# Running the feed-forward blocks of finished rows inside the attention phase of a one-core kernel

## The chip, the cores and the metric

The kernel runs on one core of a Trainium2 chip. The metric is the device time of one execution in microseconds (us), as the median of several executions. The record gives each run a state; all runs quoted here are recorded as fast. "The profile" is the record of one execution. Its "granted clock" is the share of TensorE's full clock that the chip granted. PE is the matrix engine (TensorE), PEld its weight loads, DVE the vector engine, ACT the scalar engine, POOL the GpSimd engine and SP the sync engine, which here only issue transfers (POOL also clears two buffers per batch). "L126" is line 126 of the kernel in question, so one operation has other line numbers in other kernels. PSUM is the memory that this program's matmuls write to; "bank" stands here for one PSUM buffer of 512 float32 per partition; a "ring" is the set of buffers that the operations of one tag use in turn.

"Within 2%" or "faster" comes from a ratio: the mean time of one kernel's fast runs over the mean time of the kernel before's fast runs of the same rounds. It is therefore not quite the ratio of the medians quoted beside it.

## The reference

Attention with a squared relu in place of a softmax, then a layer norm and a feed-forward block (FFN) with a residual:

```python
# q, k, v: (8 batches, 12 heads, 448 positions, 64), float32
scores = scale * np.matmul(q, k.transpose(0, 1, 3, 2))       # scale = 1/sqrt(64)
attn   = np.maximum(scores, 0.0) ** 2 / S                    # S = 448
x      = np.matmul(attn, v)  ->  reshaped to (8, 448, 768), heads side by side
xn     = (x - mean) / np.sqrt(var + 1e-06) * g_ln            # over the 768
out    = x + np.maximum(xn @ w_ch1, 0.0) @ w_ch2             # 768 -> 3072 -> 768
```

There is no exponential and no row sum. The rows of x are 8 x 448 = 3584. The FFN takes them in 7 groups of 512, so FFN group g needs batches g and g+1 (group 0 needs rows 0 to 511, which are batch 0 and a part of batch 1).

## The kernel before

It has two phases. The first runs attention for the 8 batches and writes x to a buffer in device memory. The second runs the 7 FFN groups from there. The memory pools of the second phase open when those of the first close. One head of attention is a chain over three engines:

```python
for b in range(B):
    # POOL: clear the padding of q_sb and k_sb, then load q, k, v (float32 to bf16)
    ...
    for h in range(H):
        # 8 PE transposes into two PSUM tiles of the ring "qk_ps" ...
        nc.vector.tensor_copy(q_T, q_ps)                       # DVE
        nc.vector.tensor_copy(k_T, k_ps)                       # DVE
        SC_GRP = 2
        for sg in range(n_s // SC_GRP):
            sc_ps = psum_pool_sc.tile([P, SC_GRP, S_pad], fp32, tag="sc_ps")
            ...                                                # PE: 2 score matmuls of 448 columns
            nc.scalar.activation(relu_sb[...], sc_ps[...], Relu, scale=scale_c)      # ACT
            nc.vector.tensor_mul(attn_sb[...], relu_sb[...], relu_sb[...])           # DVE: square
        # 16 PE matmuls with v, 64 columns each, then ACT or DVE copies the result to x_sb
        ...
    # SP: store x_sb to x_dram
    if b == 0:
        nc.gpsimd.dma_start(w1, moe_w_ch1...)   # 9.4 MB of float32 read, same queue as q, k, v
    elif b == 1:
        nc.gpsimd.dma_start(w2, moe_w_ch2...)
```

The FFN phase loads 512 rows of x, normalises four tiles of 128 rows (DVE, with one square root on ACT), transposes them on PE, runs 144 "up" matmuls of 512 columns (24 output tiles of 6 each; ACT applies the relu) and 192 "down" matmuls of 384 columns (8 output tiles of 24 each; DVE adds x), and stores 512 rows at once:

```python
with tc.tile_pool(name="ffn_io", bufs=3) as io_pool, ...      # opened after attention's pools closed
    for gi in range(n_m_tiles // M_GRP):
        ...  # load x_sb; per tile m: bn_stats x2, bn_aggr, Sqrt, reciprocal, tensor_scalar, tensor_mul
        ...  # PE transposes into xn_ps, ACT copies them to xn_T
        PS_GROUP = 2        # up: two output tiles per PSUM tile h1_ps
        ...  # down: o_ps; DVE adds x_sb; one store of 1536 KB per group
```

## Time and profile before

The median was 784.27 us over 6 runs. The profiled run's span is 782.2 us.

| stretch of the span | what runs | granted clock | reading |
|---|---|---|---|
| 0 to about 118 us | attention of two and a half batches | down to 0.50 (96 to 104 us) | held by loads (POOL waits 39.2 us for the weights) |
| 118.2 to 292.7 us | attention, 31.17 us per batch | 1.00 | 2.6 us per head |
| 292.7 to 315.7 us | almost nothing on PE | 0.50 | the "bubble" |
| 315.7 to 782.2 us | 7 FFN groups, about 66 us each | 0.99 | matmuls without a break inside a group |

The first view is the page's summary: span and instruction count, then busy time, share of the span and number of instructions of each engine, then the busy share of PE in 40 equal slices (in tenths) and the granted PE clock in the same slices.

```profile
span 782.2 us, 11891 instructions
PE 688.3 (88%) x5208; PEld 420.9 (54%) x5208; DVE 287.1 (37%) x657; ACT 297.6 (38%) x382; POOL 133.8 (17%) x120
PE   1878778988898881899999999999999999999996
PEclk9998869999999995899999999999999999999999
```

The "1" in the sixteenth slice is the bubble. The "886" in the clock's first slices is the start that loads hold. The next view is the table of windows of the same kernel. Its columns are start and end, length in us, then busy us and instructions of PE, PEld, DVE, ACT and POOL, granted clock, DMA share and GB/s.

```profile
92.00:106.00 14.00, 5.63 (x37) 3.62 (x37) 3.05 (x7) 1.67 (x3) 11.26 (x10) 0.56 3.90 142
118.20:292.70 174.50, 154.27 (x1866) 119.53 (x1864) 131.03 (x301) 127.56 (x169) 65.31 (x56) 1.00 1.24 73
292.70:315.70 23.00, 4.78 (x38) 3.72 (x39) 13.03 (x35) 5.86 (x11) 0.00 (x0) 0.50 0.40 133
```

In the first row PE works 5.63 of 14 us, at 0.56 of the clock. In the middle row PE reads 88% busy, which sounds full. It is not: neighbouring matmuls overlap in the record (four score matmuls, 381 ns each in the mean, take 0.78 us from the first one's start to the start of what follows, 196.19 to 196.97 us). The last row is the bubble: 4.78 us of PE work in 23 us. Because of the overlap the work is counted start to start instead. From the timeline, a head needs 8 transposes at 50 ns, 4 score matmuls at 197 ns and 16 value matmuls at 53 ns, together 2.04 us of PE. The clearing of the next q buffer marks each batch, because it waits for the last transposes of an earlier one (timeline of POOL, with start, duration, and in brackets the idle time before and what ended it):

```profile
160.81 2.66 POOL L75 MEMSET q_sb<- 128x3072 bf16 x1 [14.83 <-PE q_ps L91]
191.98 2.66 POOL L75 MEMSET q_sb<- 128x3072 bf16 x1 [14.84 <-PE q_ps L91]
```

A batch therefore takes 31.17 us, or 2.60 us per head, of which 0.56 us is waiting. One such wait is visible in the timeline of PE:

```profile
196.97 0.36 PE L94 MATMUL k_ps<-identity,k_sb 112*128 112x112 bf16 x4
197.17 0.36 PE L91 MATMUL q_ps<-identity,q_sb 112*128 112x112 bf16 x4
197.81 0.59 PE L108 MATMUL sc_ps<-q_T,k_T 128*112 128x448 bf16 x2 [0.29 <-DVE k_T L98]
```

The score matmuls stand directly behind the transposes and wait 0.29 us for the copy of k. In the FFN phase there is no wait to find inside a group: the chain of waits (start, duration, engine, what, line, count) shows whole groups running without a break.

```profile
516.31 31.24 PE h_ps L197 x144
547.55 31.21 PE o_ps L214 x192
581.50 31.12 PE h_ps L197 x144
```

144 up matmuls in 31.2 us are 217 ns each, and 192 down matmuls in 31.2 us are 162.5 ns each. Between groups 2.7 us pass here (547.55 + 31.21 to 581.50); from the second group's start to the last's, one takes 65.8 us on average.

### The profile page before, as it was taken

What the parts mean: (1) busy time and instruction counts of PE and PEld (TensorE: products, weight loads), DVE (VectorE), ACT (ScalarE), POOL (GpSimd) and SP (SyncE); (2) the same over time, 40 slices, a digit from 0 to 9 for tenths busy, and PEclk for the clock granted to TensorE, in tenths of its full rate; (3) what the DMA queues carried; (4) which work ended last, traced back from release to release, by engine and by line L of the source; (5) the groups of instructions that cost most, each with busy time, mean ns of one, the idle gap of its engine ahead of it and who ended that gap; (6) DMA issues with size and microseconds to landing.
All of it is one profiled execution on the core that took longest, in us unless ns stands there. A gap on an engine that the chain in (4) does not pass through costs nothing.

```text
span 782.2 us, 11891 instructions
## 1 busy us (share of the span) xinstructions
PE 688.3 (88%) x5208; PEld 420.9 (54%) x5208; DVE 287.1 (37%) x657; ACT 297.6 (38%) x382; POOL 133.8 (17%) x120
## 2 busy tenths in 40 slices
PE   1878778988898881899999999999999999999996
PEld 0665556766676661446445545644654554464453
DVE  0566547777777765601510230160132013010011
ACT  0565547777777662330241042043014104302300
POOL 9526184472652000000000000000000000000000
PEclk9998869999999995899999999999999999999999
DMA  9999999989979104000300030030030002002002
GB/s 87 191 158 203 170 144 50 141 70 74 133 38 115 36 2 156 1 0 1 121 1 1 15 108 0 1 122 1 1 112 10 1 1 81 1 1 80 1 1 81
DMA packets 146115, 49.13 MB, mean 63 GB/s; under 512 B 131344, under 2 KB 141584, under 8 KB 146064
## 3 DMA queue, kind: packets, MB, share of 16 engines
q0 software_dynamic: 134432, 25.96, 62.3%
q1 hardware_dynamic: 11632, 22.42, 8.6%
q8 instruction: 41, 0.67, 0.4%
q14 instruction: 10, 0.08, 0.0%
HBM read 57.80 MB, written 16.52 MB: 95 GB/s over the span
## 4 chain that ended last, share of the span: by engine, by line
PE 57%; DVE 3%; DMA 1%; ACT 1%; issue 0%; SPq 0%; DVEq 0%; ACTq 0%
PE h_ps L197 28%; PE o_ps L214 28%; DVE xn_g L183 1%; DVE xn_g L179 1%; DMA x_dram<-x_sb 1%; PE xn_ps L186 0%; ACT xn_T L188 0%; DVE stats L171 0%; DVE o_sb L220 0%; PE av_ps L129 0%; DVE stats L172 0%; SPq L141 0%; ACT L176 0%; DVE attn_sb L120 0%; DVE mv L174 0%
## 5 line engine op out<-in xcount | busy, mean ns | idle before, releaser
L197 PE MATMUL h_ps<-xn_T,w 128*128 128x512 bf16 x1008 | 221.9, 383 | 1.9 <-ACT xn_T L188 1.8
L214 PE MATMUL o_ps<-w,h_T 128*128 128x384 bf16 x1344 | 219.5, 326 | 0.0
L114 ACT ACTIVATE relu_sb<-sc_ps 112x896 bf16<-112x896 f32 x192 | 167.6, 915 | 86.5 <-PE sc_ps L108 85.9
L214 PEld LDWEIGHTS <-h_T 128*128 128x128 bf16 x1344 | 131.5, 98 | 87.6
L197 PEld LDWEIGHTS <-w 128*128 128x128 bf16 x1008 | 99.4, 99 | 122.3 <-issue 6.5
L220 DVE TENSOR_TENSOR o_sb<-o_ps,x_sb 128x384 f32<-128x384 f32 x56 | 31.2, 557 | 356.4 <-PE o_ps L214 356.4
L203 ACT ACTIVATE h_T<-h_ps 128x1024 bf16<-128x1024 f32 x84 | 85.9, 1023 | 128.4 <-PE h_ps L197 128.4
L129 PE MATMUL av_ps<-v_sb,attn_sb 112*112 112x64 bf16 x1536 | 113.9, 219 | 21.0 <-DVE attn_sb L120 20.9
L120 DVE TENSOR_TENSOR attn_sb<-relu_sb 112x896 bf16<-112x896 bf16 x192 | 118.9, 619 | 28.5 <-ACT relu_sb L114 27.4
L129 PEld LDWEIGHTS <-attn_sb 112*112 112x112 bf16 x1536 | 99.4, 134 | 42.7 <-DVE attn_sb L120 34.9
L108 PE MATMUL sc_ps<-q_T,k_T 128*112 128x448 bf16 x384 | 108.2, 381 | 5.4 <-DVE k_T L98 4.6
L188 ACT COPY xn_T<-xn_ps 128x768 bf16<-128x768 bf16 x28 | 21.1, 802 | 186.8 <-PE xn_ps L186 186.7
L91 PE MATMUL q_ps<-identity,q_sb 112*128 112x112 bf16 x384 | 41.4, 223 | 20.4 <-DMA q_sb<-in_q_dram 19.4
L94 PE MATMUL k_ps<-identity,k_sb 112*128 112x112 bf16 x384 | 45.5, 222 | 12.9 <-DMA k_sb<-in_k_dram 11.2
L108 PEld LDWEIGHTS <-k_T 128*112 128x112 bf16 x384 | 41.8, 136 | 18.0 <-DVE k_T L98 7.3
L94 PEld LDWEIGHTS <-k_sb 112*128 112x128 bf16 x384 | 32.6, 104 | 28.7 <-DMA k_sb<-in_k_dram 11.3
L97 DVE COPY q_T<-q_ps 128x448 bf16<-128x448 bf16 x96 | 36.9, 384 | 28.8 <-PE q_ps L91 27.9
L98 DVE COPY k_T<-k_ps 128x448 bf16<-128x448 bf16 x96 | 36.8, 386 | 28.8 <-PE k_ps L94 28.8
L91 PEld LDWEIGHTS <-q_sb 112*128 112x128 bf16 x384 | 27.9, 104 | 25.4 <-issue 15.5
L186 PE MATMUL xn_ps<-identity,xn_g 128*128 128x128 bf16 x168 | 14.6, 232 | 25.2 <-DVE mv L174 13.5
L79 POOL DMA_DIRECT2D k_sb<-in_k_dram x32 | 29.8, 941 | 39.2 <-DMA w<-in_moe_w_ch_dram 39.2
L79 POOL DMA_DIRECT2D v_sb<-in_v_dram x32 | 29.9, 942 | 8.1 <-DMA q_sb<-in_q_dram 7.5
(24 smaller groups left out, 213.2 us busy)
## 6 DMA issues: line engine op xcount, KB each, us to landing
out_dram<-o_sb SPq DMA_DIRECT2D x7, 1536.0 KB, 6.3
w<-in_moe_w_ch_dram POOLq DMA_DIRECT2D x2, 4608.0 KB, 32.1
q_sb<-in_q_dram POOLq DMA_DIRECT2D x32, 168.0 KB, 6.5
k_sb<-in_k_dram POOLq DMA_DIRECT2D x32, 168.0 KB, 10.2
v_sb<-in_v_dram POOLq DMA_DIRECT2D x32, 168.0 KB, 11.1
x_dram<-x_sb SPq DMA_DIRECT2D x32, 168.0 KB, 6.2
x_sb<-x_dram SPq DMA_DIRECT2D x7, 768.0 KB, 8.0
g_ln_sb<-in_moe_g_ln_dram SPq DMA_DIRECT2D x1, 384.0 KB, 3.5
```

Of the source, the lines that this page charges most:

```text
L79: nc.gpsimd.dma_start(sb[:ssz, si, :, :D], src[b, :, s0:s0 + ssz, :].rearrange("h s d -> s h d"),)
L91: nc.tensor.transpose(q_ps[:P, si * ST:si * ST + ssz], q_sb[:ssz, si, h, :], identity[:ssz, :ssz])
L94: nc.tensor.transpose(k_ps[:P, si * ST:si * ST + ssz], k_sb[:ssz, si, h, :], identity[:ssz, :ssz])
L97: nc.vector.tensor_copy(q_T, q_ps)
L98: nc.vector.tensor_copy(k_T, k_ps)
L108: nc.tensor.matmul(sc_ps[:ssz, j, :S], k_T[:, si * ST:si * ST + ssz], q_T[:, :S], start=True, stop=True,)
L114: nc.scalar.activation(relu_sb[:ST, sg * SC_GRP:(sg + 1) * SC_GRP, :], sc_ps[:ST, :, :S], mybir.ActivationFunctionType.Relu, scale=scale_c,)
L120: nc.vector.tensor_mul(attn_sb[:ST, sg * SC_GRP:(sg + 1) * SC_GRP, :], relu_sb[:ST, sg * SC_GRP:(sg + 1) * SC_GRP, :], relu_sb[:ST, sg * S ...
L129: nc.tensor.matmul(av_ps[:msz, mi, :], attn_sb[:ssz, si, m0:m0 + msz], v_sb[:ssz, si, h, :], start=(si == 0), stop=(si == n_s - 1),)
L197: nc.tensor.matmul(h1_ps[:, j, :], w1[:, ki, ni * P:(ni + 1) * P], xn_T[:, ki, :], start=(ki == 0), stop=(ki == K1 - 1),)
L203: nc.scalar.activation(h1_T[:, ng * PS_GROUP:(ng + 1) * PS_GROUP, :], h1_ps, mybir.ActivationFunctionType.Relu,)
L214: nc.tensor.matmul(o_ps, h1_T[:, ki, m * P:(m + 1) * P], w2[:, ki, j * dh:(j + 1) * dh], start=(ki == 0), stop=(ki == K2 - 1),)
```

## The change

Its intent is to use the attention phase's waits: as soon as a group's 512 rows exist, its FFN is cut into 32 slices (24 up, 8 down), and after each head as many are emitted as spread 32 over 12 heads. FFN group g runs from batch g+2 on. The bubble and the gaps between groups should vanish as well. The buffers of both phases are now open at once; attention gives up buffers, squares in place, and takes its scores one tile at a time, so that scores and up outputs can share a ring of four PSUM banks. The normalised-x transposes share the q/k ring, and the down outputs the value ring.

```diff
     with tc.tile_pool(name="attn_io", bufs=2) as io_pool, \
-         tc.tile_pool(name="attn_t", bufs=6) as t_pool, \
+         tc.tile_pool(name="attn_t", bufs=3) as t_pool, \
...
-         tc.tile_pool(name="attn_ps_sc", bufs=2, space=bass.MemoryType.PSUM) as psum_pool_sc, \
-         tc.tile_pool(name="attn_tmp", bufs=4) as tmp_pool:
+         tc.tile_pool(name="attn_ps_sc", bufs=4, space=bass.MemoryType.PSUM) as psum_pool_sc, \
+         tc.tile_pool(name="attn_tmp", bufs=2) as tmp_pool, \
+         tc.tile_pool(name="ffn_io", bufs=2) as ffn_io_pool, \
+         tc.tile_pool(name="ffn_h1", bufs=1) as h1_pool, \
+         tc.tile_pool(name="ffn_tmp", bufs=2) as ffn_tmp_pool:
+        slices = []
+        def queue_ffn_group(gi):
+            ...                                   # load x_sb, as before
+            def norm(m): ...                      # as before, xn_g now one buffer
+            def turn(m):
+                xn_ps = psum_pool.tile([P, K1, P], bf16, tag="qk_ps")
+                ...
+            PS_GROUP = 1
+            def up(ng):
+                h1_ps = psum_pool_sc.tile([P, PS_GROUP, M_FREE], fp32, tag="sc_ps")
+                ...                               # 6 matmuls of 512 columns, relu on ACT
+            def down(m, j):
+                o_ps = psum_pool.tile([P, S_pad], fp32, tag="av_ps")
+                ...                               # 24 matmuls of 384 columns, add on DVE
+                nc.sync.dma_start(out_flat[...], o_sb)     # 192 KB, 56 times
+            return norm, turn, body
...
-                attn_sb = tmp_pool.tile([P, n_s, S], bf16, tag="attn_sb")
-                SC_GRP = 2
+                attn_sb = relu_sb
+                SC_GRP = 1
...
+                if h == 0 and next_gi[0] <= (b * S) // M_FREE - 1:
+                    group = queue_ffn_group(next_gi[0])
+                    next_gi[0] += 1
+                if group and H_LN < h <= H_LN + M_GRP:
+                    group[1](h - H_LN - 1)                  # turn
+                if group and H_LN <= h < H_LN + M_GRP:
+                    with tc.issue_after(r_ins.ins), tc.issue_after(m_ins.ins):
+                        group[0](h - H_LN)                  # norm, heads 2 to 5
+                if group and h == H_LN + M_GRP:
+                    slices.extend(group[2])
+                    group = None
+                credit[0] = credit[0] + 32 / H if slices else 0.0
+                while slices and credit[0] >= 1.0:
+                    slices.pop(0)()
+                    credit[0] -= 1.0
...
+        while next_gi[0] < n_m_tiles // M_GRP:              # the last group, after attention
+            norm, turn, body = queue_ffn_group(next_gi[0])
+            ...
+        while slices:
+            slices.pop(0)()
```

## The prediction

> What bounds the kernel now. The chain of waits gives PE 57% of the span, nearly all of it the FFN matmuls that end last. The table of windows splits the run: to 118 us, attention of two and a half batches held by DMA and low clock (0.5 near 100 us); 118 to 293 us, attention at clock 1.0, about 2.6 us per head; 293 to 316 us, PE almost idle (last x store, x load, first layer norm), clock 0.5; from 316 us, seven FFN groups of about 65 us. [...] 144 up matmuls take 31.2 us (217 ns each for 512 columns) and 192 down matmuls 31.2 us (162.5 ns each for 384)[...].
>
> Attention, start to start in the timeline, needs per head of PE 8 transposes at 50 ns, 4 score matmuls at 197 ns and 16 value matmuls at 53 ns: 2.04 us. Measured 2.6 us, so some 0.56 us per head is waiting on the chain transpose, copy, score, relu, square, value; ACT (2.0 us) and DVE (2.2 us) are nearly as full.
>
> The change runs FFN group g inside attention of batch g+2, 32 slices per 12 heads. Up to 293 us it could fill 66 heads x 0.56 = 37 us of waits; it removes most of the 23 us bubble and some 15 us between groups. At most 75 us, near 710 us.
>
> What it costs. Scores go one tile at a time: a 448-wide relu is 0.53 us by my estimate (line through 373, 915 and 1023 ns), so ACT pays 0.2 to 0.3 us more per head, DVE as much; neither becomes the limit (ACT about 47 and DVE about 46 us per batch against PE about 85 to 100). By the instruction order of the changed kernel, scores still come right after 3 k and 4 q transposes, so the k copy (0.38 us) is exposed as now (0.29 us idle in the timeline of before), and only 2 matmuls stand between the relu/square chain and each value matmul. By hand, with those durations, about 0.8 us of PE wait remains per head in the up phase; in the down phase the normalised-x transposes share two PSUM buffers with q and k, and cost about 4 us per batch. Together 50 to 60 us.
>
> Sum: 118 us start (DMA-held, unchanged) + 5 to 10 (first group: four heads each wait for a layer norm) + 66 x 2.04 = 135 + FFN matmuls 437 + transposes 8 + waits 50 to 60 + last group's norm 5 + tail 4 = 762 to 777. My waits are worst cases: I shade down.
>
> Predicted 762 us, 8 in 10 within 724 to 796; faster by over 2%: 0.55; within 2%: 0.37; slower: 0.08.
>
> What would show it right: the first 118 us alike; PE's granted clock near 1.0 from about 130 us to the end; the 23 us idle stretch gone; PE waits named by value weights on the square (DVE), score on the k copy, normalised-x transposes on DVE, some 0.6 to 0.9 us per head; ACT and DVE busy sums up by some 30 us each.
>
> What would make it wrong: if PE fills the waits well (waits under 0.4 us per head), near 730 us. If the slices delay each head's chain, or relu of an FFN slice stands before a score's relu in ACT's order, 800 us.

The sum: it came to 762 to 777 us, and its FFN term of 437 us is 7 groups at the 62.4 us measured.

## The result and the profile after

The changed kernel takes 771.45 us (8 runs, 769.17 to 773.52) against 784.96 us; the ratio is 0.9827, with a 95% interval of 0.9812 to 0.9841. That is within 2%: a gain of 1.7%, some 13 us, of up to 75 us that the prediction thought there to win. The profiled run's span is 770.6 us. The page's summary of the kernel after:

```profile
span 770.6 us, 12452 instructions
PE 694.5 (90%) x5208; PEld 414.9 (54%) x5208; DVE 328.8 (43%) x849; ACT 322.3 (42%) x658; POOL 133.8 (17%) x120
PE   0877867999999999999999999999999999999998
PEclk9997966899999999999999999999999999999999
```

The bubble is gone and the clock reads 9 (0.9 or more) from the ninth slice to the end; the mean from 144 to 770 us is 1.00. But slices five to eight of the clock now read "9668" where they read "8699" before: the slow start lasts longer. The windows say what is in it:

```profile
120.00:136.70 16.70, 13.55 (x112) 10.21 (x111) 13.93 (x37) 9.86 (x20) 0.00 (x0) 0.60 1.83 56
258.00:355.40 97.40, 92.58 (x696) 54.57 (x696) 43.90 (x111) 42.21 (x87) 16.32 (x15) 1.00 0.46 54
```

From 120 to 136.7 us the clock is 0.60 and DVE is busy 13.93 of 16.7 us: there the first group's layer norms stand among the heads of batch 2. (A low clock was recorded beside an idle PE, 0.50 in the bubble of the kernel before, and here beside a PE that reads busy 13.55 of 16.7 us, in pieces between short waits; what sets it no run here isolates.) The first up matmul starts only at 136.7 us, behind seven heads of batch 2 (heads 0 to 6). From the first score matmul of head 0 to that up matmul it is 32.5 us:

```profile
104.16 1.74 PE L201 MATMUL sc_ps<-q_T,k_T 128*112 128x448 bf16 x4 [0.39 <-DVE k_T L191]
136.69 4.79 PE L126 MATMUL h_ps<-xn_T,w 128*128 128x512 bf16 x12
```

In the kernel before, the same seven heads take 19.5 us (timeline of PE, 104.69 to 124.14 us, the end of head 6's value matmuls). The second row of the windows is one steady batch with an FFN group inside. Its length can be read off the batch marks, as before:

```profile
257.98 2.66 POOL L168 MEMSET q_sb<- 128x3072 bf16 x1 [80.04 <-PE q_ps L184]
355.40 2.66 POOL L168 MEMSET q_sb<- 128x3072 bf16 x1 [80.04 <-PE q_ps L184]
```

It is 97.4 us. In the kernel before, an attention batch and an FFN group one after the other take 31.2 + 65.8 = 97.0 us. So in the steady state the interleaving wins nothing at all. The PE work in 97.4 us is 12 x 2.04 + 62.4 + about 1.4 for the group's 24 transposes = 88.3 us, which leaves 9.1 us of waits, 0.76 us per head: more than the 0.56 us per head of the kernel before. (PE "busy" reads 92.58 of 97.4 us, 95%.) The timeline of PE shows one head:

```profile
269.30 0.31 PE L187 MATMUL k_ps<-identity,k_sb 112*128 112x112 bf16 x3
269.44 0.36 PE L184 MATMUL q_ps<-identity,q_sb 112*128 112x112 bf16 x4
270.09 0.96 PE L201 MATMUL sc_ps<-q_T,k_T 128*112 128x448 bf16 x4 [0.29 <-ACT h_t L132]
...
271.12 0.59 PE L126 MATMUL h_ps<-xn_T,w 128*128 128x512 bf16 x2
271.55 0.24 PE L223 MATMUL av_ps<-v_sb,relu_sb 112*112 112x64 bf16 x1
271.62 0.60 PE L126 MATMUL h_ps<-xn_T,w 128*128 128x512 bf16 x2
...
272.85 0.86 PE L223 MATMUL av_ps<-v_sb,relu_sb 112*112 112x64 bf16 x13
273.54 2.54 PE L126 MATMUL h_ps<-xn_T,w 128*128 128x512 bf16 x11
```

The score matmuls still follow the transposes directly, so a wait of 0.29 us is still there; here the profile puts its end down to the relu of an FFN tile (at 270.10 us), which came 0.06 us after the copy of k. Only seven of the head's 18 up matmuls lie between the scores and the bulk of the value matmuls, where relu and square are awaited, and they come two at a time with a single value matmul between. The other eleven run in one piece after the values, where PE had nothing to wait for. What PE waits for in this batch (engine, what and line, then us in total, times, longest) is:

```profile
PEld L223 <- DVE relu_sb L213: 10.8, 40, 0.9
PEld L201 <- DVE k_T L191: 3.3, 7, 0.6
PE sc_ps L201 <- ACT h_t L132: 2.2, 7, 0.5
PE xn_ps L112 <- DVE q_T L190: 1.2, 2, 0.6
```

The weight loads of the value matmuls wait for squares, as they did before, and the scores now also wait for the relu of an FFN tile to free a bank of the shared ring (third line); the fourth line is the x transposes, which wait for the copy of q. Waits of PEld and PE overlap each other (PEld waits 10.8 us for squares here, while PE's own steps lose 1.7 us before value matmuls, as counted next), so the lines do not add up to the 9.1 us.

Where PE really lost the 9.1 us shows when every step from one matmul's start to the next is taken, less that matmul's own 50, 53, 197, 217, 162.5 or (x transpose) 58 ns. Before scores stand 3.7 us, before value matmuls only 1.7, before x transposes 1.4, before up matmuls 1.4, before the transposes of q and k 0.8. In a batch of the kernel before, counted in the same way, the loss is 4.5 us before value matmuls and 2.3 before scores. So the slices do cover most of the wait for squares. What they do not cover is the wait at the scores, and the shared rings add waits of their own.

Where the time went, from the two profiles:

| term | before | after | change |
|---|---|---|---|
| bubble between attention and FFN | 23.0 | 0 | -23 |
| the seven heads up to the end of the first group's norms | 19.5 | 32.5 | +13 |
| PE waits from there on (65 heads; after: counted start to start to the last matmul) | 65 x 0.56 = 36 | 53 | +17 |
| gaps of the first six FFN groups beyond 62.4 us of matmuls | 396.8 - 374.4 = 22 | 8 (transposes) | -14 |
| last matmul to end (one 1536 KB store, 6.3 us from issue to landing in the median, or 192 KB ones, 1.9 us) | about 7 | about 3 | -4 |

The terms sum to -11 us; the spans differ by 11.6 us.

### The profile page after: what moved, and what is told of

It reads as the page before. It is cut to its first block, busy times and chain, and to the rows that moved or that the text cites. A ratio compares the mean times of both kernels' runs of the same rounds, so it can differ in the third digit from the quotient of the medians.

```text
span 770.6 us, 12452 instructions
## 1 busy us (share of the span) xinstructions
PE 694.5 (90%) x5208; PEld 414.9 (54%) x5208; DVE 328.8 (43%) x849; ACT 322.3 (42%) x658; POOL 133.8 (17%) x120
## 4 chain that ended last, share of the span: by engine, by line
PE 75%; DMA 11%; ACT 5%; DVE 5%; POOL 2%; issue 1%; SPq 0%; POOLq 0%; ACTq 0%
PE h_ps L126 28%; PE o_ps L144 28%; PE av_ps L223 8%; PE sc_ps L201 8%; DMA w<-in_moe_w_ch_dram 4%; DMA q_sb<-in_q_dram 4%; ACT h_t L132 3%; DMA k_sb<-in_k_dram 3%; ACT relu_sb L207 1%; PE xn_ps L112 1%; PE k_ps L187 1%; DVE q_T L190 1%; PE q_ps L184 1%; POOL q_sb L172 1%; DVE o_sb L150 1%
## 5 line engine op out<-in xcount | busy, mean ns | idle before, releaser
L126 PE MATMUL h_ps<-xn_T,w 128*128 128x512 bf16 x1008 | 245.3, 381 | 0.9
L207 ACT ACTIVATE relu_sb<-sc_ps 112x448 bf16<-112x448 f32 x384 | 177.6, 550 | 124.3 <-PE sc_ps L201 123.9
L144 PE MATMUL o_ps<-w,h_t 128*128 128x384 bf16 x1344 | 226.4, 326 | 0.0
L144 PEld LDWEIGHTS <-h_t 128*128 128x128 bf16 x1344 | 128.8, 99 | 78.9
L213 DVE TENSOR_TENSOR relu_sb<-relu_sb 112x448 bf16<-112x448 bf16 x384 | 144.4, 389 | 59.1 <-ACT relu_sb L207 51.3
L132 ACT ACTIVATE h_t<-h_ps 128x512 bf16<-128x512 f32 x168 | 100.3, 597 | 154.0 <-PE h_ps L126 150.5
L223 PEld LDWEIGHTS <-relu_sb 112*112 112x112 bf16 x1536 | 111.1, 134 | 77.7 <-DVE relu_sb L213 70.4
L223 PE MATMUL av_ps<-v_sb,relu_sb 112*112 112x64 bf16 x1536 | 140.6, 218 | 11.2 <-DVE relu_sb L213 9.3
L150 DVE TENSOR_TENSOR o_sb<-o_ps,x_sb 128x384 f32<-128x384 f32 x56 | 31.2, 557 | 177.3 <-PE o_ps L144 177.3
L168 POOL MEMSET q_sb<- 128x3072 bf16 x8 | 21.3, 2665 | 280.8 <-PE q_ps L184 280.8
L187 PEld LDWEIGHTS <-k_sb 112*128 112x128 bf16 x384 | 34.2, 102 | 34.2 <-DMA k_sb<-in_k_dram 11.6
L172 POOL DMA_DIRECT2D k_sb<-in_k_dram x32 | 29.7, 936 | 38.7 <-DMA w<-in_moe_w_ch_dram 38.3
L230 ACT CAST x_sb<-av_ps 112x256 bf16<-112x256 f32 x48 | 18.0, 375 | 35.8 <-PE av_ps L223 35.8
```

Source lines behind the costliest of these rows:

```text
L126: nc.tensor.matmul(h1_ps[:, j, :], w1[:, ki, ni * P:(ni + 1) * P], xn_T[:, ki, :], start=(ki == 0), stop=(ki == K1 - 1),)
L132: nc.scalar.activation(h1_T[0][:, ng * PS_GROUP:(ng + 1) * PS_GROUP, :], h1_ps, mybir.ActivationFunctionType.Relu,)
L144: nc.tensor.matmul(o_ps[:, :dh], h1_T[0][:, ki, m * P:(m + 1) * P], w2[:, ki, j * dh:(j + 1) * dh], start=(ki == 0), stop=(ki == K2 - 1),)
L150: nc.vector.tensor_add(o_sb, o_ps[:, :dh], x_sb[:, m, j * dh:(j + 1) * dh],)
L172: nc.gpsimd.dma_start(sb[:ssz, si, :, :D], src[b, :, s0:s0 + ssz, :].rearrange("h s d -> s h d"),)
L187: nc.tensor.transpose(k_ps[:P, si * ST:si * ST + ssz], k_sb[:ssz, si, h, :], identity[:ssz, :ssz])
```

## The experiments

Twelve kernels ran. All gave correct results. The table has them in order; the text below goes by question.

| kernel | what it is | median us | ratio to before (95%) |
|---|---|---|---|
| attn_only | before, with attention's new buffers and tile sizes alone | 777.6 | 0.9906 (0.9875 to 0.9937) |
| bubble_only | after, without interleaving | 751.59 | 0.9567 (0.9543 to 0.9591) |
| split | after, with a PSUM ring of their own for up outputs | 758.11 | 0.9656 (0.9640 to 0.9672) |
| start3 | after, each group one batch later | 765.29 | 0.9750 (0.9725 to 0.9775) |
| before_w24 | before, weight loads later | 773.67 | 0.9858 (0.9808 to 0.9907) |
| bubble_w24 | bubble_only, weight loads later | 749.63 | 0.9553 (0.9533 to 0.9573) |
| after_w23 | after, weight loads later | 758.94 | 0.9681 (0.9652 to 0.9710) |
| split_w23 | split, weight loads later, norms of the last groups between down slices | 742.06 | 0.9470 (0.9442 to 0.9499) |
| bubble_wend | bubble_only, weight loads behind all others | 728.06 | 0.9288 (0.9260 to 0.9315) |
| split_xn | split_w23, x transposes out of the q/k ring | 736.67 | 0.9386 (0.9355 to 0.9417) |
| before_wend | before, weight loads behind all others | 765.42 | 0.9752 (0.9721 to 0.9783) |
| bubble_spread | bubble_wend, first group's norms spread over four batches | 732.94 | 0.9331 (0.9312 to 0.9350) |

### Do the narrow score tiles and fewer buffers cost time? (attn_only)

```diff
-         tc.tile_pool(name="attn_t", bufs=6) as t_pool, \
+         tc.tile_pool(name="attn_t", bufs=3) as t_pool, \
-         tc.tile_pool(name="attn_ps_sc", bufs=2, ...
+         tc.tile_pool(name="attn_ps_sc", bufs=4, ...
-         tc.tile_pool(name="attn_tmp", bufs=4) as tmp_pool:
+         tc.tile_pool(name="attn_tmp", bufs=2) as tmp_pool:
-                attn_sb = tmp_pool.tile([P, n_s, S], bf16, tag="attn_sb")
-                SC_GRP = 2
+                attn_sb = relu_sb
+                SC_GRP = 1
```

> The kernel before with only the attention parts of the change: scores one tile at a time, four one-bank score buffers, squares in place, t pool 3, tmp pool 2; the FFN stays behind attention. Theory A (these parts cost nothing by themselves, attention stays at about 2.6 us per head): 785 us, within 5. Rival B (the added fixed time of narrower ACT and DVE instructions, some 0.3 us per head, is on the chain): 96 heads x 0.3 = up to 29 us more, 800 us or above.

(The 0.3 us of rival B is the prediction's estimate from ACT's 373, 915 and 1023 ns.) It took 777.6 us, so both expectations missed: the parts that were thought a price are a gain of about 8 us. A batch takes 29.95 us instead of 31.17. The four edits were made together, so which of them gained it is not shown. The trace suggests that the finer tiles let the chain overlap: the value matmuls' wait for squares fell from 20.9 to 11.2 us over the run, and ACT's wait for scores from 85.9 to 68.1 us. The price was small, because durations of neighbouring ACT instructions overlap in the record: the mean of a 448-wide relu reads 550 ns, but four in a row take 1.84 us together (after, 123.04 us), an overlap of (4 x 0.55 - 1.84) / 3 = 0.12 us each, against 1.72 us for the two 896-wide ones (before, 200.60 us).

### Does interleaving pay, or only the removed bubble? (bubble_only)

This is the changed kernel without any slice inside attention. Only group 0 is loaded, normalised and transposed there, in batch 7; the groups follow attention, and each group's norms stand between the down slices of the one before.

```diff
-                if h == 0 and next_gi[0] <= (b * S) // M_FREE - 1:
+                if h == 0 and b == B - 1:
-                credit[0] = credit[0] + 32 / H if slices else 0.0
+                credit[0] = 0.0
 # after attention, in place of the two final loops:
+        while slices or next_gi[0] < n_m_tiles // M_GRP:
+            nxt = queue_ffn_group(next_gi[0]) ...
+            for i, piece in enumerate(todo):
+                piece()
+                if nxt and left < 8 and left % 2 == 1:      # left: slices still to come
+                    nxt[0](3 - left // 2); nxt[1](3 - left // 2)
```

> The changed kernel without interleaving: only group 0 is loaded, normalised and transposed during the last batch, all FFN matmuls come after attention, each next group's norm between the down slices. Theory I (a batch with a group inside costs 97.4 us in the trace of after, about 31.2 + 65.1 = 96.3 one after the other in the trace of before, so interleaving wins nothing and all the gain is the removed 23 us bubble and the gaps between groups): 750 to 765 us, below after. Rival (the slices do fill attention's waits, so taking them away loses most of the gain): 775 to 785.

It took 751.59 us, inside the range of the theory that interleaving wins nothing, and 20 us faster than the changed kernel. The timeline of PE shows an FFN group of this kernel, with the next group's transposes placed between down slices at no visible gap:

```profile
366.52 31.24 PE L126 MATMUL h_ps<-xn_T,w 128*128 128x512 bf16 x144
397.60 4.06 PE L144 MATMUL o_ps<-w,h_t 128*128 128x384 bf16 x24
401.50 0.50 PE L112 MATMUL xn_ps<-identity,xn_g 128*128 128x128 bf16 x6
...
430.14 10.09 PE L126 MATMUL h_ps<-xn_T,w 128*128 128x512 bf16 x46
```

A group takes 430.14 - 366.52 = 63.6 us, which is its matmuls and its transposes. And a batch of attention alone, read off POOL's marks in the same kernel:

```profile
159.61 2.66 POOL L168 MEMSET q_sb<- 128x3072 bf16 x1 [12.52 <-PE q_ps L184]
189.56 2.66 POOL L168 MEMSET q_sb<- 128x3072 bf16 x1 [12.51 <-PE q_ps L184]
```

That is 29.95 us. One after the other the same parts take 93.6 us, where the changed kernel's interleaving takes 97.4: it costs 3.8 us per batch, and five and a half batches of that make 21 us, about the 20 us. This kernel too pays for the first group's norms: heads 0 to 6 of batch 7 take 31.2 us, where those of batch 3 take 18.8. From the mark that precedes its last two batches (219.5 us) to the first up matmul (302.5 us) it takes 83.0 us, where two plain batches take 59.9; some 5 us of this difference (my estimate from bubble_spread below, whose last batch has no norm) are not the norms, because the mark falls at the last transposes of a batch and the scores and values of the last heads still follow. (The expectations quote 96.3 us for the kernel before in series; 97.0 is the right figure, from the mean of all group starts.) Interleaving did not pay; the reason is in the order on PE above, and in the next experiment.

### Is it the shared ring? (split, split_xn)

In split the four banks are divided: two for scores, two for up outputs.

```diff
-         tc.tile_pool(name="attn_ps_sc", bufs=4, ...
+         tc.tile_pool(name="attn_ps_sc", bufs=2, ...
-                h1_ps = psum_pool_sc.tile([P, PS_GROUP, M_FREE], fp32, tag="sc_ps")
+                h1_ps = psum_pool_sc.tile([P, PS_GROUP, M_FREE], fp32, tag="h1_ps")
```

> The changed kernel with its four one-bank PSUM buffers split in two rings, two for scores and two for FFN up outputs (tag h1_ps). In the instruction order FFN matmuls then stand between the copy of k and the scores, and between scores and values. Theory P (the shared ring fixes the order and so leaves about 9 us of PE waits per batch): waits fall to 3 to 5 us per batch, some 5.5 batches, so 740 to 752 us. Rival C (the head's own chain or ACT and DVE hold it): 768 us or more, with waits on the square growing since only two score banks are there.

It took 758.11 us, between the two ranges. The shared ring was a real cost, as the window of one batch (two marks apart) and its waits show:

```profile
263.40:357.20 93.80, 91.84 (x698) 53.54 (x697) 43.87 (x111) 42.41 (x87) 16.33 (x15) 1.00 0.72 56
```

```profile
PEld L223 <- DVE relu_sb L213: 5.7, 19, 0.6
```

The batch falls from 97.4 to 93.8 us, and the wait for squares is halved (10.8 to 5.7 us). But 93.8 us is only what the same parts take in series (93.6). Its remaining 5.5 us of waits (93.8 - 88.3) are as many as 12 heads have without any FFN work among them (29.95 - 24.5 = 5.5). Net, the slices fill nothing, even with rings apart. Counted start to start, the wait only moves: before value matmuls twelve heads alone lose 4.1 us and split 0.6, but before scores they lose 1.6 us and split 4.0, and the x transposes and those of q and k add 1.2. In split an up matmul stands directly before 27 of the batch's 48 score matmuls (before 1 in the changed kernel); what holds the scores there is not shown. At the start split loses some of its gain: its seven heads with the first norms take 38.3 us, against 32.7 in the changed kernel.

The prediction had also charged 4 us per batch to the transposes of x that share the q/k ring. split_xn is split_w23 with these moved to the ring of the up outputs:

```diff
-                xn_ps = psum_pool.tile([P, K1, P], bf16, tag="qk_ps")
+                xn_ps = psum_pool_sc.tile([P, K1, P], bf16, tag="h1_ps")
```

> split_w23 with the normalised-x transposes put into the ring of the FFN up outputs instead of the two buffers of q and k. Theory X (in the down phase the transposes of x wait for the q copy to free a buffer and the next k transposes wait for ACT's copy of x, my prediction's 4 us per batch): batches shrink from 93.8 to about 91.5 us, 728 to 734 us in all. Rival (these waits are the chain through DVE and come back at the scores and squares): 738 to 746 us.

It took 736.67 us, between the two again. The batch fell from 93.8 to 93.3 us only, so that sharing is worth about half a microsecond per batch, not 4; the waits for squares stayed (6.0 us). On the changed kernel itself this was not run. There the start-to-start count above puts 1.4 us per batch before the x transposes.

### Why does the first group cost 13 us? (start3, after_w23, bubble_spread)

The trace of the changed kernel at one of the heads with a norm, PE's scores and what DVE does between them:

```profile
122.38 1.74 PE L201 MATMUL sc_ps<-q_T,k_T 128*112 128x448 bf16 x4 [0.48 <-DVE k_T L191]
122.44 0.48 DVE L102 TENSOR_SCALAR xn_g<-x_sb,mv,rstd 128x768 bf16<-128x768 bf16 x1
122.95 0.96 DVE L106 TENSOR_TENSOR xn_g<-xn_g,g_ln_sb 128x768 bf16<-128x768 bf16 x1
...
123.82 1.49 DVE L213 TENSOR_TENSOR relu_sb<-relu_sb 112x448 bf16<-112x448 bf16 x4
...
127.64 1.74 PE L201 MATMUL sc_ps<-q_T,k_T 128*112 128x448 bf16 x4 [0.48 <-DVE k_T L191]
```

The head takes 5.26 us instead of 2.5. The norm's DVE instructions (two statistics, aggregate, reciprocal, scale, multiply: 0.55 + 0.54 + 0.20 + 0.15 + 0.48 + 0.96 = 2.9 us) stand in the same queue as the squares and copies that PE waits for. In later batches FFN slices of the group before keep PE busy meanwhile (92.58 of 97.4 us in the batch above); the first group has none before it. Three experiments looked for the cause. (Their expectations speak of six heads; there are seven, heads 0 to 6.)

start3 moves every group one batch later, so that the first norms come when the loads are over (and it places the last groups' norms between down slices, as bubble_only does).

```diff
-                if h == 0 and next_gi[0] <= (b * S) // M_FREE - 1:
+                if h == 0 and next_gi[0] <= ((b - 1) * S) // M_FREE - 1:
```

> The changed kernel with every FFN group one batch later (group g in batch g+3), the last groups behind attention with their norms between down slices. Theory S (in batch 2 the first group's norms meet a PE at half clock and no FFN work to fill, costing about 10 us over attention alone, six heads took 33 us): the start is 10 us cheaper, and interleaving one batch less loses nothing: 758 to 766 us. Rival (the start costs nothing special, or one batch less of interleaving loses its fill): 771 us or more.

It took 765.29 us, inside the expected range, but for another reason than expected. The window shows the same slow heads again, one batch later:

```profile
150.00:165.00 15.00, 11.82 (x95) 8.60 (x92) 13.02 (x36) 9.49 (x20) 0.00 (x0) 0.61 1.74 73
```

Clock 0.61 and DVE at 13.02 of 15 us, though the preceding batch ran undisturbed; the seven heads took 30.8 us (135.25 to 166.02), where plain ones take 18.8. So the weight loads do not cause it. The gain probably comes from one interleaved batch fewer and from shorter gaps at the end, which this run neither shows nor separates.

after_w23 is the changed kernel with the weight loads moved in the source behind the loads of batches 2 and 3 (see below).

```diff
+            if b == 2:
+                nc.gpsimd.dma_start(w1, ...)
+            elif b == 3:
+                nc.gpsimd.dma_start(w2, ...)
```

> The changed kernel with the weight loads moved behind batches 2 and 3. Theory W with theory S (half clock in batch 2 comes from the DMA hold just before, and the six heads before the first FFN slice took 33 us instead of 15): first FFN slice near 110 to 115 us instead of 137, total 746 to 752 us. Rival (only the hold goes, the slow first norms stay): 754 to 760 us. If w1 lands too late: first slice waits for it and nothing is won.

It took 758.94 us, the rival's range. The first group's heads were slow again (82.5 to 127 us), now with a still worse wait: DVE stood 13.0 us at the first statistics, because the store and the load of x took 8.57 and 11.35 us, to 104.5 us, while w1 was still under way (POOL's next load waited for it until 100.17 us). The squares of attention stood behind the statistics in DVE's queue, and PE's value matmuls waited 13.9 us for them.

bubble_spread, the last run, asks whether four norms in a row are the trouble. It starts from bubble_wend (below), where batches 6 and 7 with the first group's norms take 197.1 to 278.3 us, 21 us more than two plain batches (59.9 us), some 5 us of it the end of attention itself.

```diff
-                if h == 0 and b == B - 1:
+                if h == 0 and b == 3:
-                if group and H_LN < h <= H_LN + M_GRP:
-                    group[1](h - H_LN - 1)
-                if group and H_LN <= h < H_LN + M_GRP:
+                if group and h == 8:
+                    group[1](b - 3)
+                if group and h == 4:
                     with tc.issue_after(r_ins.ins), tc.issue_after(m_ins.ins):
-                        group[0](h - H_LN)
+                        group[0](b - 3)
```

> The version with both weight loads behind all others (728.06 us), in which only the first FFN group's four layer norms are moved: from four heads in a row of batch 7 to one head each of batches 3, 4, 5 and 6. Theory D, the first group is dear because four heads in a row carry about 2.9 us of norm work each on DVE on top of about 2.2 us of attention's own, so that a head takes 5.3 us instead of 2.5 and the granted clock falls: one norm alone costs at most its own 2.9 us, the last two batches, which took 81 us instead of 60, return to about 60, the clock stays at 1.0, and the time is 714 to 720 us. Rival, the loss is the end of attention itself (last head, last store and load, first transposes) or each norm costs its 5 us wherever it stands: the time stays at 724 us or more.

It took 732.94 us, and so went against theory D: spread out, the norms cost more, not less. Batch 7, now without norms, takes 28.7 us from its first score matmul to the first up matmul, against 46.1 in bubble_wend, so in a row the four norms cost 17.4 us. Batches 3 to 6, with one norm each, take 142.1 us against 119.9 in bubble_wend, 22.2 more. POOL's marks show three of them:

```profile
108.26 2.66 POOL L168 MEMSET q_sb<- 128x3072 bf16 x1 [10.82 <-PE q_ps L191]
144.61 2.66 POOL L168 MEMSET q_sb<- 128x3072 bf16 x1 [15.73 <-PE q_ps L191]
179.40 2.66 POOL L168 MEMSET q_sb<- 128x3072 bf16 x1 [17.02 <-PE q_ps L191]
```

The intervals are 36.35 and 34.79 us, and the next one is 34.52, instead of 29.95: one norm costs 4.6 to 6.4 us in each of them. The granted clock was 0.91 from 150 to 190 us, within the second and third of these intervals, but 1.00 from 220 to 262 us, in the fourth batch with a norm, which took 35.6 us all the same (first scores of batch 6 to first scores of batch 7); so the low clock around the norms is a companion, not the main cause. The first norm is the dearest, and the trace shows one reason: a table load of 1.28 us stands on ACT just before the first square root, the only one after the load at the program's start, and DVE waits 1.14 us for that square root with attention's squares behind.

```profile
128.72 1.28 ACT L99 ACT_TABLE_LOAD   x1
130.34 0.16 DVE L100 RECIPROCAL rstd<-rstd 128x1 f32<-128x1 f32 x1 [1.14 <-ACT rstd L99]
```

The changed kernel has the same load at 115.55 us, and DVE waits 1.5 us there. Of the 5 us of the others, 2.9 are DVE's own work, which fits an engine that is busy 32.61 of 38 us in plain attention (bubble_only, 217 to 255 us). The other 2 us were not taken apart; the instruction order in this head, where the norm's square root on ACT and the copy of k on DVE follow each other, is a candidate that no run here tests.

### How much of the start is the weights' loads? (the runs named w)

In the kernel before, POOL's timeline shows what a later load of attention waited for:

```profile
91.50 0.93 POOL L79 DMA_DIRECT2D k_sb<-in_k_dram  x1 [20.85 <-DMA w<-in_moe_w_ch_dram]
```

w2, queued ahead of the loads of a batch, held POOL for 20.9 us. The prediction had taken the first 118 us as given. Four kernels move the weight loads; the first two are before_w24 and bubble_w24.

```diff
 # after the loads of q, k and v of batch b
+            if b == 2:
+                nc.gpsimd.dma_start(w1, moe_w_ch1...)
+            elif b == 4:
+                nc.gpsimd.dma_start(w2, moe_w_ch2...)
 # and the two loads after the stores of batches 0 and 1 removed
```

> The kernel before with only the two weight loads moved: queued behind the q, k and v loads of batches 2 and 4 instead of behind those of batches 0 and 1. Theory W (the two 32 us weight loads hold the loads of batches 1 and 2, leaving PE idle near 52 to 64 and 92 to 108 us, at half clock): about 17 us less, 766 to 770 us, granted clock 1.0 from 25 to 290 us. Rival (attention's own chain sets these batches, DMA only looks busy): 782 to 786 us.

> bubble_only with the same move of the weight loads. If the two savings are independent: 751.6 - 17 = about 735 us (730 to 740). If the start's saving is eaten by a later DMA hold: 745 or more.

They took 773.67 and 749.63 us, both misses. The order on POOL's queue was not that of the source: w1 came behind batch 2's loads, but w2 behind batch 3's, not batch 4's as the expectation words it. The hold moved with them: in before_w24, POOL waited 27.9 us on the weights and the clock was 0.50 from 150 to 160 us. The same move on the kernel with rings apart:

> split with the same move and with the last group's norms put between down slices. If savings add: 758.1 - 20 - 4 = about 734 us (728 to 742). It also tells whether interleaving with split rings (93.8 us per batch with a group inside) is any better than one after the other (93.6 us in bubble_only): theory I says split_w23 and bubble_w24 end within 6 us of each other.

It took 742.06 us, the upper edge of its range, and 7.6 us less than bubble_w24, where theory I had said within 6. POOL waited 7.8 us for the weights here and 31.9 us in bubble_w24, so the pair does not settle whether interleaving with rings apart pays; without the move, split is 6.5 us slower than bubble_only. Then the order was made binding, behind the last load of batch 7:

```diff
-                    nc.gpsimd.dma_start(
+                    ld = nc.gpsimd.dma_start(
...
+            if b == 7:
+                with tc.issue_after(ld.ins):
+                    nc.gpsimd.dma_start(w1, ...)
+            if b == 7:
+                with tc.issue_after(ld.ins):
+                    nc.gpsimd.dma_start(w2, ...)
```

> bubble_only with both weight loads held behind the last q, k and v loads by an ordering edge. In the runs before this one the scheduler had moved them up on POOL's queue, behind batches 2 and 3 in all four, so holds came back near 115 and 150 us. With nothing left behind them they can hold nothing: theory W says all batches run at about 30 us from 23 us on, 751.6 - 17 to 20 = 732 to 736 us, granted clock 1.0 from 25 us to the end of attention. Rival (the q, k and v loads alone already set the first batches): 745 us or more.

> The kernel before with nothing changed but both weight loads held behind the last q, k and v loads. It splits bubble_wend's gain: if the start's saving is the same without the other changes, 785 - 20 to 24 = 761 to 765 us; if it needs the finer attention, 770 or more.

bubble_wend took 728.06 us, better than expected, and is the best version found: about 43 us faster than the changed kernel and 55 us faster than the kernel before of its own rounds (783.17). The window that read 0.56 of the clock and 5.63 us of PE before reads in bubble_wend:

```profile
92.00:106.00 14.00, 13.08 (x153) 10.15 (x151) 11.73 (x37) 10.74 (x26) 1.87 (x2) 1.00 2.60 155
```

before_wend took 765.42 us, at the edge of its range: the order of two transfers alone gives the kernel before 19 us, more than the whole change gave (13.5 us). The changed kernel cannot take this order, since its first slices need w1 in batch 2; after_w23 is as far as it was tried.

## Why the prediction was right or wrong

The time was inside the range (771.45 us in 724 to 796, point 762). The more likely direction, faster by over 2%, did not come true: the gain was 1.7%.

- **The sum by hand was right, and the shading was wrong.** It gave 762 to 777 us, and the prediction went to its low end because "my waits are worst cases". Term by term, the profile shows: 13 us for the first group against 5 to 10; the heads at 2.04 us, the FFN matmuls and the transposes as summed; PE waits 53 us against 50 to 60; last group's norm 1 to 2 us against 5; tail 3.4 us against 4. That the sum held is in part luck: the first group was sized too low, the last group's norm and the x transposes too high.
- **The mis-sized term is "5 to 10 (first group: four heads each wait for a layer norm)".** It measured 13 us (32.5 us for seven heads that took 19.5). The mechanism was named rightly and the size was too small. Four norms at 13 us are 3.3 us each, not the 1.3 to 2.5 us that "5 to 10" implies; spread among heads without FFN slices they cost 4.6 to 6.4 us each (bubble_spread). "Neither becomes the limit" was right over a batch, where DVE is busy 43.90 of 97.4 us, and wrong in these heads, where it is busy 13.93 of 16.7 us.
- **"PE's granted clock near 1.0 from about 130 us" was wrong by about 14 us**: 0.60 up to 136.7 us, and full from about 144 us.
- **"Some 0.6 to 0.9 us per head" of PE waits was right**: 0.76. The waits named are in the profile too, but the first of them, value weights on the square, costs PE little: 1.7 of the 9.1 us stand before value matmuls, 3.7 before scores. That this reading leaves no gain in the steady state (0.76 against 0.56 us in the kernel before) was in the numbers of the prediction, but not drawn from it.
- **"The normalised-x transposes share two PSUM buffers with q and k, and cost about 4 us per batch" was not borne out.** Taking them out won 0.5 us per batch (split_xn, on a variant), and the trace of the changed kernel shows 1.4 us per batch before these transposes. The ring that mattered was the other one, shared by scores and up outputs: 3.6 us per batch (split).
- **"ACT pays 0.2 to 0.3 us more per head, DVE as much" was right as busy time, wrong as cost.** ACT's sum rose by 24.7 us and DVE's by 41.7 us (30 each were predicted), but attention's edits alone made the kernel before 8 us faster (attn_only); that the narrow tiles did it, by overlapping and starting the chain earlier, is argued from the trace.
- **"It removes most of the 23 us bubble" was right in the letter.** The bubble is gone, but the first group's norms, which were part of it, came back inside attention: 12 to 13 us over the same seven heads in the changed kernel, start3, bubble_only and bubble_wend, and more in split and after_w23.
- **"118 us start (DMA-held, unchanged)" was right for this change**, and hid the cheapest gain: 19 us (before_wend).

Shown by runs: that a batch with a group inside takes about as long as the two in series or longer (93.3 to 97.4 us against 93.6), that the shared ring costs 3.6 us per batch, that the norms' cost does not come from the weight loads nor from standing in a row, and that the weight loads' place is worth 19 us to the kernel before. Not shown: that another order of the slices would fill the waits. The scheduler sets that order; only split changed it, as a by-product, and there the waits moved to the scores.

## What to carry to other kernels

Before interleaving two phases, compare what it can fill with what the phases take one after the other, and look at where in the engine's queue the filler will stand: filler behind the last instruction of a chain fills no wait inside that chain (here eleven of a head's 18 up matmuls), and filler inside it can move the wait to the next place (in split, from the value matmuls to the scores). When a bubble is removed by moving its work earlier, charge that work to the engine it moves onto, at the place where it moves: here the vector engine was busy 32.61 of 38 us in plain attention, and 23 us of bubble became 13 us of slow heads. The two large loads that were not needed yet belonged behind the small ones that were (19 us in before_wend), in the order that the queue really had; the trace showed that order, the source did not.
